# One decode step of attention and feed-forward on one core: GpSimd weighs and halves 32 of 128 rows of each value tile, VectorE sums the 16 that are left, and several matmuls become fewer and wider

## The chip, the core and the metric

The kernel runs on one core of a Trainium2 chip, in float32 throughout. The core has a matmul engine (TensorE, PE in the profile), VectorE (DVE), ScalarE (ACT), GpSimd (POOL) and SyncE (SP), which here only issues transfers, and 16 DMA engines that bring data from device memory to the on-chip memory SBUF. Results of matmuls go to PSUM. The metric is the device time of one execution in microseconds (us); lower is better.

## The reference

One token for each of four sequences goes through a block with adaptive layer norm: six modulation vectors come from a conditioning vector `c`; attention with 32 heads over a cache of 4096 keys and values per head; then a feed-forward with SiLU.

```python
mod = (_silu(c) @ w_mod).reshape(c.shape[0], 6, 1, -1)
sa, ca, ga, sb, cb, gb = (mod[:, i] for i in range(6))
h = _layernorm(x) * (1 + ca) + sa
q = (h @ wq).reshape(B, Sq, H, Dh).transpose(0, 2, 1, 3)
scores = einsum("bhqd,bhkd->bhqk", q, k_cache) * (Dh ** -0.5)
o = einsum("bhqk,bhkd->bhqd", softmax(scores), v_cache)
x = x + ga * (o.transpose(0, 2, 1, 3).reshape(B, Sq, H * Dh) @ wo)
h = _layernorm(x) * (1 + cb) + sb
x = x + gb * (_silu(h @ w1) @ w2)
```

Here B is 4, H is 32, the model is 512 wide, Dh is 128 and the cache has 4096 positions, so keys and values are 4 x 32 x 4096 x 128 numbers each, 268 MB each. The hidden layer is 1792 wide.

## The kernel before

The work on the cache is cut into 32 steps n, each for one sequence b = n mod 4 and one group t of four heads. A step has a key tile and a value tile of 128 partitions x 128 rows x 128 numbers, 8.4 MB each. A partition holds 128 consecutive positions of one head; "a row" below is one of these positions, 128 numbers in each partition.

**Transfers.** The pool `kv` has three buffers of the size of a tile. All big transfers go through the queue of SyncE, in the order `wm`, `wq`, k0, v0, k1, v1, ..., k31, v31, `wo`, and then `w1` and `w2` together in one buffer (`w12`). Each takes the buffer that was filled three places earlier, so k(n+1) waits until the work on v(n-1) is done, v(n+1) waits for the work on k(n), `wo` for the work on v30 and `w12` for the work on k31. SyncE issues in order: a transfer whose buffer isn't free holds back those behind it. `wo`, `w1` and `w2` come in pieces (`fetch`, L80).

**One step** (the loop at L353). The key tile is multiplied by the query in place: GpSimd does the first `NA` = 56 rows with a copy of the query in SBUF (`qw`), VectorE the other 72 with the query in PSUM (`qb`) (`mult`, L251). VectorE then adds up each row (`red`, L256), first its own 72 rows, then those of GpSimd; this gives 128 scores per partition in `sc`. Row maximum (`rowmax` L259, `bmax` L263, `negmax` L268) and exponential (`softexp` L275, on ScalarE) follow. GpSimd spreads the exponentials into two zero-padded tables `pz` (L281), 16 groups of four rows each, and TensorE multiplies them with the value tile (`pv`, L288): 32 matmuls of four rows, 512 columns, which run four at a time on four strips of 32 columns of the array. `po` collects two sequences b and b+1. The profile counts each float32 matmul as two passes, so a `pv` is 64.

`gather` (L306) masks `po` and adds up its four parts by four matmuls into `od`; it runs for the first pair in the step with b = 2 and for the second in the next step with b = 0. `spread` (L330) divides by the softmax sum and writes the result as weights `oz`, in steps with b = 0. `make_qb(n + 1)` (L240) makes the next query tile by ScalarE, a matmul and a copy. The engines get their instructions in exactly the order in which the code is written.

**The last step** (n = 31) has its key tile loaded in two halves, and GpSimd and VectorE multiply half by half, 28 and 36 rows each (L373 to L378).

**The end** (L401 to L442). `project` multiplies `oz` by `wo` into `accp`: for each t and each of four parts r there are four matmuls of 128 columns. The second pair's last `gather` and `spread` stand between its parts. Then come the gate and residual (L415, L416), a layer norm, 16 matmuls with `w1`, the SiLU, 56 matmuls with `w2` in the order of its six pieces, two operations for gate and residual, and the output's transfer. `busy` issues matmuls whose result isn't used.

**The start** (L177 to L236). `mods` makes the modulation vectors by 96 matmuls of 128 columns; the query projection with `wq` follows.

## Time and profile before

| | |
|---|---|
| time, median of 3 runs | 1323.78 us (1323.75 to 1323.86) |
| the profiled execution's own time | 1323.81 us |
| its span in the profile | 1321.9 us |
| busy: PE, DVE, ACT, POOL | 398.0, 923.3, 44.7, 533.5 us |
| mean granted TensorE clock | 0.636 of full speed |
| read from device memory | 567.30 MB |

The profile shows one execution, with times in us from the start of the span; the execution's own time has 1.9 us around that span. A group in the profile is a set of instructions of one source line (L252 is line 252), engine and operation, written as result <- operands; its columns are the busy time in all and the mean ns of one, then the engine's idle time ahead of them and what ended it. "PE" rows are matmul passes, "PEld" rows their weight loads, "SPq" rows the transfers that SyncE issues. A row of the timeline has the start, the duration from first to last, the engine, the line, the operation with its tiles and how many; square brackets give the idle time just before. The chain that ended last is followed back from the last instruction of the program.

### The profile page before, as it was taken

Reading aid. Unit: us, or ns where it says so; the run is one execution under the profiler, and the core shown is the slowest. Engines: PE = TensorE matmul, PEld = TensorE weight load, DVE = VectorE, ACT = ScalarE, POOL = GpSimd, SP = SyncE. Lnnn points to the kernel's source line nnn. Section 1 sums busy time; section 2 is a strip of 40 time slices with the busy share of each in tenths; the row PEclk is TensorE's granted clock in tenths of the full one; section 3 lists DMA queues with packets and bytes.
Section 4 is the critical chain, followed back from the end, with each engine's and each line's share of the span. In section 5 each row is a group of like instructions: output and inputs, shape, how many; then the busy total and the mean of one; then the engine's idle time right before and its main releaser. Section 6 shows DMA issues by size and latency. Waiting matters only on the chain.

```text
span 1321.9 us, 7059 instructions
## 1 busy us (share of the span) xinstructions
PE 398.0 (30%) x2998; PEld 145.4 (11%) x2998; DVE 923.3 (70%) x335; ACT 44.7 (3%) x146; POOL 533.5 (40%) x111
## 2 busy tenths in 40 slices
PE   3321223323123333212333321323332132333146
PEld 2100001101010010101001010100100010010014
DVE  1267877766887666788667678776668876676971
ACT  1100000000000000000000000000000000000000
POOL 1234455433445533354543334454334445433540
PEclk9765566665566666566666656666655666665569
DMA  9999999999999999999999999999999999999998
GB/s 414 441 418 439 442 419 438 439 424 431 441 430 429 437 436 427 436 436 429 435 433 435 428 435 438 426 435 440 423 435 444 418 437 444 419 437 439 420 422 330
DMA packets 12287, 567.76 MB, mean 430 GB/s; under 512 B 1440, under 2 KB 1504, under 8 KB 2272
## 3 DMA queue, kind: packets, MB, share of 16 engines
q1 hardware_dynamic: 12048, 567.29, 99.4%
q8 instruction: 23, 0.38, 0.1%
q14 instruction: 8, 0.07, 0.0%
q0 software_dynamic: 128, 0.01, 0.0%
q10 hardware_dynamic: 80, 0.02, 0.0%
HBM read 567.30 MB, written 0.01 MB: 429 GB/s over the span
## 4 chain that ended last, share of the span: by engine, by line
DMA 32%; issue 31%; POOL 25%; PE 7%; DVE 4%; POOLq 0%; SPq 0%; DVEq 0%
DMA k<-in_A_k_cache_dram 26%; POOL k L252 24%; PE po L297 6%; DMA w<-in_B_w_dram 3%; DMA wq<-in_A_wq_dram 3%; DVE sc L257 3%; DVE k L252 1%; POOL pz L281 1%; PE q L221 1%; PE mx L231 0%; POOLq L281 0%; DVE o L308 0%; PE po L434 0%; PE mx L265 0%; SPq L123 0%
## 5 line engine op out<-in xcount | busy, mean ns | idle before, releaser
L252 POOL TENSOR_TENSOR k<-k,qw 128x7168 f32<-128x7168 f32 (+1 forms) x33 | 491.4, 14893 | 290.1 <-DMA k<-in_A_k_cache_dram 264.7
L257 DVE TENSOR_REDUCE sc<-k 128x72 f32<-128x9216 f32 (+2 forms) x66 | 554.4, 8422 | 1.1
L252 DVE TENSOR_TENSOR k<-k,q 128x9216 f32<-128x9216 f32 (+1 forms) x33 | 312.3, 9463 | 309.3 <-DMA k<-in_A_k_cache_dram 300.1
L297 PE MATMUL po<-v,pz 128*32 128x512 f32 x2048 | 292.1, 735 | 48.6 <-POOL pz L281 47.9
L281 POOL TENSOR_TENSOR pz<-sc,hm 128x256 f32<-128x256 f32 x64 | 37.9, 612 | 458.1 <-ACT sc L279 445.7
L265 PE MATMUL mx<-ident,rm 128*128 128x128 f32 x32 | 14.5, 453 | 531.2 <-DVE rm L261 531.2
L314 PE MATMUL od<-o,spick 128*128 128x128 f32 x128 | 32.3, 431 | 293.4 <-DVE o L308 293.4
L297 PEld LDWEIGHTS po<-v,pz 128*32 128x32 f32 x2048 | 71.2, 132 | 248.2 <-issue 191.9
L265 PEld LDWEIGHTS mx<-ident,rm 128*128 128x128 f32 x32 | 5.8, 181 | 538.8 <-issue 332.1
L314 PEld LDWEIGHTS od<-o,spick 128*128 128x128 f32 x128 | 27.7, 319 | 296.5 <-DVE o L308 296.3
L279 ACT ACTIVATE sc<-sc,nm 128x128 f32<-128x128 f32 x32 | 12.8, 401 | 891.9 <-DVE nm L273 891.9
L270 DVE TENSOR_REDUCE hx<-mx 128x4 f32<-128x128 f32 x32 | 9.3, 291 | 19.7 <-PE mx L265 19.7
L247 ACT ACTIVATE qw<-q 128x128 f32<-128x128 f32 x32 | 8.9, 277 | 302.9 <-PE q L244 302.9
L308 DVE TENSOR_TENSOR o<-po,jm 128x512 f32<-128x512 f32 x16 | 10.9, 680 | 8.4 <-PE po L297 8.4
L244 PE MATMUL q<-qm,blk 128*128 128x128 f32 x64 | 15.6, 326 | 1.5 <-ACT qm L242 1.5
L183 PE MATMUL q<-wm 128*32 128x128 f32 x192 | 9.2, 375 | 20.3 <-DVE wm L170 20.3
L244 PEld LDWEIGHTS q<-qm,blk 128*128 128x128 f32 x64 | 9.5, 188 | 27.0 <-issue 25.1
L242 ACT ACTIVATE qm<-qn,sel 128x128 f32<-128x128 f32 x32 | 12.4, 387 | 0.9 <-DMA xg<-in_A_x_dram 0.9
L221 PE MATMUL q<-wq,wm 128*32 128x512 f32 x64 | 9.3, 748 | 7.4 <-DMA wq<-in_A_wq_dram 7.4
L183 PEld LDWEIGHTS q<-wm 128*32 128x32 f32 x192 | 7.8, 153 | 21.0 <-DVE wm L170 20.3
L261 DVE TENSOR_REDUCE rm<-sc 128x1 f32<-128x128 f32 x32 | 9.1, 284 | 0.9
L167 DVE SCALAR_TENSOR_TENSOR wm<-wm 128x128 f32<-128x128 f32 x1 | 0.3, 291 | 12.3 <-ACT wm L166 12.3
(79 smaller groups left out, 104.2 us busy)
## 6 DMA issues: line engine op xcount, KB each, us to landing
k<-in_A_k_cache_dram SPq DMA_DIRECT2D x2, 4096.0 KB
wm<-in_w_mod_dram SPq DMA_DIRECT2D x1, 6144.0 KB
wo<-in_A_wo_dram SPq DMA_DIRECT2D x1, 4096.0 KB
wo<-in_A_wo_dram SPq DMA_DIRECT2D x1, 2048.0 KB
wo<-in_A_wo_dram SPq DMA_DIRECT2D x2, 1024.0 KB, 35.2
...
```

Source lines behind the costliest of these rows:

```text
L183: nc.tensor.matmul(p[W * g : W * (g + 1), u, :], csT[:, k, :], wmt[:, k, o : o + P], start=k == 0, stop=k == NK - 1,)
L221: nc.tensor.matmul(pq[i][W * g : W * (g + 1), :], hT[:, k, :], wqt[:, k, ch * CW : (ch + 1) * CW], start=k == 0, stop=k == NK - 1,)
L242: nc.scalar.activation(m, qn, AF.Copy, scale=sel[:, n : n + 1])
L244: nc.tensor.matmul(p, blk.rearrange("p i x -> p (i x)"), m, start=True, stop=True)
L252: eng.tensor_mul(kt[n][:, lo:hi, :], kt[n][:, lo:hi, :], src[n].unsqueeze(1).to_broadcast([P, hi - lo, Dh]))
L257: nc.vector.tensor_reduce(sc[n][:, lo:hi], kt[n][:, lo:hi, :], axis=AX.X, op=ALU.add)
L265: nc.tensor.transpose(p, nm[n].to_broadcast([P, P]), ident)
L279: nc.scalar.activation(sc[n], sc[n], AF.Exp, bias=nm[n], accum_out=rs[t][:, b : b + 1])
L281: nc.gpsimd.tensor_mul(pz[h][:, : HG * W].rearrange("p (g x) -> p g x", g=HG)[:, :, E:].rearrange("p g (i j) -> p g i j", i=HP), sc[n][:, ...
L297: nc.tensor.matmul(po[t, q][W * g : W * (g + 1), :], pz[h][:, o : o + W], vt[n][:, JJ * j : JJ * (j + 1), :].rearrange("p j d -> p (j d)") ...
L308: nc.vector.tensor_mul(o, po[t, q].rearrange("p (j d) -> p j d", j=JJ), jm.unsqueeze(2).to_broadcast([P, JJ, Dh]))
L314: nc.tensor.matmul(od[t], spick[:, 2 - 2 * q : 2 - 2 * q + P], o[:, j, :], start=(q == 0 and j == 0), stop=(q == 1 and j == JJ - 1),)
```

## The change

On the value side, GpSimd multiplies the first `NV` = 32 rows of a value tile by their exponentials in place and adds rows 16 to 31 to rows 0 to 15 (`vmult`, `fold`). In the next step VectorE adds up these 16 rows with a strided view (`vsum`), and one matmul puts the sum into `po`. `pv` then has 24 matmuls instead of 32, and `pz` holds 24 groups. The last step (`first(n)` is 0) does without this. On the key side GpSimd has 48 rows instead of 56; in the last step it has 32 in each half.

`make_qb` makes four query tiles at once with one matmul of 512 columns every fourth step. `gather` adds its four parts on VectorE and has one matmul. `project` has one matmul of 512 columns for each t and r, the four r on four strips; the strips are then added up by four matmuls with `sel`, for which `accp` is copied by VectorE and ScalarE. `mods` is likewise turned to 512 columns with a masking step behind it. The table for the SiLU is loaded ahead by a one-column activation, and one `busy` matmul goes.

```diff
-    NA = 56
+    NA = 48
+    NL = 64
+    NV = 32
...
     def mods(dsts, i):
...
+        n = len(dsts)
+        p = psum([P, D], "q", 2)
+        for k in range(NK):
+            for u in range(n):
+                nc.tensor.matmul(
+                    p[W * u : W * (u + 1), :], csT[:, k, :], wmt[:, k, (i + u) * D : (i + u + 1) * D],
+                    start=k == 0, stop=k == NK - 1,
+                )
+        z = psum([P, n, P], "q", 2)
+        r = W * n
+        for g in range(G):
+            m = mm[:r, g % 2, :n, :]
+            nc.vector.tensor_mul(
+                m, p[:r, g * P : (g + 1) * P].unsqueeze(1).to_broadcast([r, n, P]),
+                hm[:r, :n].unsqueeze(2).to_broadcast([r, n, P]),
+            )
+            nc.tensor.matmul(z[W * g : W * (g + 1), :, :], sel[:r, :], m, start=True, stop=True)
...
     def make_qb(n):
-        m = work.tile([P, Dh], F32, tag="lnu", name=f"qm{n}", bufs=1)
-        nc.scalar.activation(m, qn, AF.Copy, scale=sel[:, n : n + 1])
-        p = psum([P, Dh], "q", 2)
-        nc.tensor.matmul(p, blk.rearrange("p i x -> p (i x)"), m, start=True, stop=True)
-        qb[n] = p
+        if n % B == 0:
+            m = work.tile([P, B, Dh], F32, tag="o", name=f"qm{n}", bufs=1)
+            for b in range(B):
+                nc.scalar.activation(m[:, b, :], qn, AF.Copy, scale=sel[:, n + b : n + b + 1])
+            p = psum([P, B, Dh], "q", 2)
+            nc.tensor.matmul(p, blk.rearrange("p i x -> p (i x)"), m, start=True, stop=True)
+            for b in range(B):
+                qb[n + b] = p[:, b, :]
...
+    def first(n):
+        return NV // JJ if n < N - 1 else 0
+
+    def vmult(n):
+        if first(n):
+            nc.gpsimd.tensor_mul(
+                vt[n][:, :NV, :], vt[n][:, :NV, :], sc[n][:, :NV].unsqueeze(2).to_broadcast([P, NV, Dh])
+            )
+            fold(nc.gpsimd, n, NV // 2)
+
+    def fold(eng, n, m):
+        eng.tensor_add(vt[n][:, :m, :], vt[n][:, :m, :], vt[n][:, m : 2 * m, :])
+
+    def vsum(n):
+        t, b = divmod(n, B)
+        q, a = divmod(b, 2)
+        s = work.tile([P, Dh], F32, tag="lnu", name="vs", bufs=1)
+        nc.vector.tensor_reduce(s, vt[n][:, : NV // 2, :].rearrange("p j d -> p d j"), axis=AX.X, op=ALU.add)
+        o = (1 - a) * E
+        nc.tensor.matmul(po[t, q][0:W, 0:Dh], hs[:, o : o + W], s, start=False, stop=a == 1)
...
-        for j in range(NG):
+        f = first(n)
+        for j in range(f, NG):
...
-        for j in range(JJ):
-            nc.tensor.matmul(
-                od[t], spick[:, 2 - 2 * q : 2 - 2 * q + P], o[:, j, :],
-                start=(q == 0 and j == 0), stop=(q == 1 and j == JJ - 1),
-            )
+        s = work.tile([P, Dh], F32, tag="lnu", name="s", bufs=1)
+        nc.vector.tensor_reduce(s, o.rearrange("p j d -> p d j"), axis=AX.X, op=ALU.add)
+        nc.tensor.matmul(od[t], spick[:, 2 - 2 * q : 2 - 2 * q + P], s, start=q == 0, stop=q == 1)
...
-                for g in range(G):
-                    nc.tensor.matmul(
-                        accp[W * g : W * g + B, :], oz[:, t, r, :], wot[:, t, r, g * P : (g + 1) * P],
-                        start=(t == 0 and r == 0), stop=(t == NT - 1 and r == R - 1),
-                    )
+                nc.tensor.matmul(
+                    accp[W * r : W * r + B, :], oz[:, t, r, :], wot[:, t, r, :],
+                    start=t == 0, stop=t == NT - 1,
+                )
...
             make_qb(n + 1)
+            if n:
+                vsum(n - 1)
             red(n, NA, NJ)
         else:
             for lo in (0, NJ // 2):
-                mid, hi = lo + NA // 2, lo + NJ // 2
+                mid, hi = lo + NL // 2, lo + NJ // 2
                 mult(nc.gpsimd, qw, n, lo, mid)
                 mult(nc.vector, qb, n, mid, hi)
+                if lo == 0:
+                    vsum(n - 1)
                 red(n, mid, hi)
-            red(n, NJ // 2, NJ // 2 + NA // 2)
...
-        red(n, 0, NA if n + 1 < N else NA // 2)
+        if n + 1 < N:
+            red(n, 0, NA)
+        else:
+            for lo in (0, NJ // 2):
+                red(n, lo, lo + NL // 2)
...
+        vmult(n)
         pv(n)
...
-    nc.vector.tensor_mul(x1, ga, accp)
+    ac = work.tile([P, D], F32, tag="o", name="ac", bufs=1)
+    nc.vector.tensor_copy(ac[:, : D // 2], accp[:, : D // 2])
+    nc.scalar.activation(ac[:, D // 2 :], accp[:, D // 2 :], AF.Copy)
+    xa = psum([P, P], "mx", 2)
+    for g in range(G):
+        nc.tensor.matmul(xa[W * g : W * (g + 1), :], sel, ac[:, g * P : (g + 1) * P], start=True, stop=True)
+    nc.vector.tensor_mul(x1, ga, xa)
     nc.vector.tensor_add(x1, x1, xg)
     busy(4)
     layernorm_mod(hg, x1, sb, cb1)
+    nc.scalar.activation(th[:, 0:1], x1[:, 0:1], AF.Tanh)
...
-    busy(6)
+    busy(5)
```

Two places show how the order of instructions changes. The first is VectorE from the softmax of step 30 to the row maximum of step 31; k31 and v30 are the key tile of step 31 and the value tile of step 30, sc31 the scores, q the query in PSUM, vs the sum of the 16 rows. Before:

```order
L273 TENSOR_REDUCE nm30_2309<-hx30_2306 128x1
L252 TENSOR_TENSOR k31_2281<-k31_2281,q_2289 128x4608
L257 TENSOR_REDUCE sc31_2354<-k31_2281 128x36
L252 TENSOR_TENSOR k31_2281<-k31_2281,q_2289 128x4608
L257 TENSOR_REDUCE sc31_2354<-k31_2281 128x36
L257 TENSOR_REDUCE sc31_2354<-k31_2281 128x28 x2
L261 TENSOR_REDUCE rm31_2363<-sc31_2354 128x1
```

The same place on VectorE after the change:

```order
L292 TENSOR_REDUCE nm30_2081<-hx30_2078 128x1
L271 TENSOR_TENSOR k31_2055<-k31_2055,q_1879 128x4096
L326 TENSOR_REDUCE vs_2123<-v30_2027 128x128
L276 TENSOR_REDUCE sc31_2120<-k31_2055 128x32
L271 TENSOR_TENSOR k31_2055<-k31_2055,q_1879 128x4096
L276 TENSOR_REDUCE sc31_2120<-k31_2055 128x32 x3
L280 TENSOR_REDUCE rm31_2132<-sc31_2120 128x1
```

The sum over v30 now stands behind the first multiplication of step 31, ahead of every reduction and of the second multiplication.

The second place is GpSimd from the key rows of step 30 to the end of step 31; pz0 and pz1 are the two tables, qw the query in SBUF, hm a constant mask. Before:

```order
L252 TENSOR_TENSOR k30_2222<-k30_2222,qw30_2231 128x7168
L281 TENSOR_TENSOR pz0_118<-sc30_2284,hm_101 128x16x16
L281 TENSOR_TENSOR pz1_119<-sc30_2284,hm_101 128x16x16
L252 TENSOR_TENSOR k31_2281<-k31_2281,qw31_2291 128x3584 x2
L281 TENSOR_TENSOR pz0_118<-sc31_2354,hm_101 128x16x16
L281 TENSOR_TENSOR pz1_119<-sc31_2354,hm_101 128x16x16
```

The same place on GpSimd after the change:

```order
L271 TENSOR_TENSOR k30_2003<-k30_2003,qw30_2008 128x6144
L302 TENSOR_TENSOR pz0_118<-sc30_2058,hm_101 128x8x16
L302 TENSOR_TENSOR pz1_119<-sc30_2058,hm_101 128x16x16
L314 TENSOR_TENSOR v30_2027<-v30_2027,sc30_2058 128x4096
L320 TENSOR_TENSOR v30_2027<-v30_2027 128x2048
L271 TENSOR_TENSOR k31_2055<-k31_2055,qw31_2061 128x4096 x2
L302 TENSOR_TENSOR pz0_118<-sc31_2120,hm_101 128x16x16
L302 TENSOR_TENSOR pz1_119<-sc31_2120,hm_101 128x16x16
```

The weighing and the halving of v30 (4096 and 2048 elements per partition) now stand between the tables of step 30 and the key rows of step 31; each earlier step has the same two instructions at this place.

More of the change, by code (lines that the diff above doesn't have):

```diff
@@ L107 @@
     tmp = s0.take(P)
+    mm = s0.take(2, 4, P)
     csT, hT = s0.take(NK, W), s0.take(NK, W)
@@ L160 @@
         nc.gpsimd.memset(t, 0.0)
+    hs = const.tile([P, W + E], F32, name="hs")
+    nc.vector.memset(hs, 0.0)
+    nc.vector.tensor_copy(
+        hs[:, E : 2 * E].rearrange("p (i j) -> p i j", i=HP), hm.unsqueeze(2).to_broadcast([P, HP, JJ])
+    )
     oz = const.tile([P, NT, R, B], F32, name="oz")
@@ L177, in mods @@
     def mods(dsts, i):
-        p = psum([P, 4, P], "q", 2)
-        for u in range(len(dsts)):
-            for k in range(NK):
-                for g in range(G):
-                    o = (i + u) * D + g * P
-                    nc.tensor.matmul(
-                        p[W * g : W * (g + 1), u, :], csT[:, k, :], wmt[:, k, o : o + P],
-                        start=k == 0, stop=k == NK - 1,
-                    )
+        n = len(dsts)
[15 more added lines that the diff above has]
+            nc.tensor.matmul(z[W * g : W * (g + 1), :, :], sel[:r, :], m, start=True, stop=True)
         for u, d in enumerate(dsts):
             nc.scalar.activation(
-                d, p[:, u, :], AF.Copy,
+                d, z[:, u, :], AF.Copy,
                 scale=0.25 if i + u == 5 else 0.5, bias=1.0 if i + u in (1, 4) else 0.0,
@@ L240, in make_qb @@
     def make_qb(n):
[L241 to L245 removed]
+        if n % B == 0:
[6 more added lines that the diff above has]
+                qb[n + b] = p[:, b, :]
         qw[n] = work.tile([P, Dh], F32, tag="qw", name=f"qw{n}")
[L247 removed]
+        nc.scalar.activation(qw[n], qb[n], AF.Copy)
     sc, nm, po, rs = {}, {}, {}, {}
@@ L300, in pv @@
                 vt[n][:, JJ * j : JJ * (j + 1), :].rearrange("p j d -> p (j d)"),
-                start=(a == 0 and j < G), stop=(a == 1 and j >= NG - G),
+                start=(a == 0 and j < f + G), stop=(a == 1 and j >= NG - G and (g > 0 or not f)),
             )
@@ L337, in spread @@
         nc.vector.tensor_copy(oz[:, t], ot[:, :, :B])
-    accp = psum([P, P], "acc", 1)
+    accp = psum([P, D], "acc", 1)
     nc.vector.memset(accp, 0.0)
@@ L344, in project @@
             for r in range(R):
-                for g in range(G):
-                    nc.tensor.matmul(
-                        accp[W * g : W * g + B, :], oz[:, t, r, :], wot[:, t, r, g * P : (g + 1) * P],
-                        start=(t == 0 and r == 0), stop=(t == NT - 1 and r == R - 1),
-                    )
+                nc.tensor.matmul(
+                    accp[W * r : W * r + B, :], oz[:, t, r, :], wot[:, t, r, :],
+                    start=t == 0, stop=t == NT - 1,
+                )
     make_qb(0)
@@ L405 @@
     project(NT - 1, NT)
+    x1, hg, y = (s2.take(P) for _ in range(3))
+    h2T, hid, th, hidT = s2.take(NK, W), s2.take(FG), s2.take(FG), s2.take(NI, W)
     idle = psum([P, P], "q", 2)
@@ L411, in busy @@
             nc.tensor.matmul(idle, ident, qn, start=True, stop=True)
-    x1, hg, y = (s2.take(P) for _ in range(3))
-    h2T, hid, th, hidT = s2.take(NK, W), s2.take(FG), s2.take(FG), s2.take(NI, W)
-    nc.vector.tensor_mul(x1, ga, accp)
+    ac = work.tile([P, D], F32, tag="o", name="ac", bufs=1)
[5 more added lines that the diff above has]
+    nc.vector.tensor_mul(x1, ga, xa)
     nc.vector.tensor_add(x1, x1, xg)
```

11 lines of the change are left out of this document (6 added, 5 removed).

## The prediction

> **What bounds the kernel now.** I first read the head of the page for the load of the DMA engines (the row "DMA" is their busy share in 40 slices, the last row the queue of SyncE).
>
> ```profile
> span 1321.9 us, 7059 instructions
> DMA  9999999999999999999999999999999999999998
> q1 hardware_dynamic: 12048, 567.29, 99.4%
> ```
>
> The queue keeps the 16 engines busy for 99.4% of the span, in every stretch. 567.29 MB in 1321.9 us is 429 GB/s. No compute engine sets the pace as long as this queue never runs dry. Next, the end of the chain that ended last (start, duration, what).
>
> ```profile
> 1304.65 13.11 DMA w<-in_B_w_dram
> 1317.81 0.47 PE po L434 x8
> ```
>
> The last piece of `w2` lands at 1317.8, eight matmul passes follow, and the span ends 3.62 us after the last of them ends (1318.28). The change neither removes a byte nor touches these last steps. So nothing here can become faster by more than a fraction of a microsecond, and two questions remain: does the queue still never run dry, and does the compute of the last step still end before the last piece lands?
>
> The timeline tells how much room there is: one step in the middle (step 14 starts at 601), the start, and the step ahead of the last.
>
> ```profile
> 38.38 9.33 PE L221 MATMUL q<-wq,wm 128*32 128x512 f32 x64 [7.36 <-DMA wq<-in_A_wq_dram]
> 47.77 0.33 SPq L82 DMA_DIRECT2D v<-in_A_v_cache_dram  x1
> 57.81 9.75 DVE L252 TENSOR_TENSOR k<-k,q 128x9216 f32<-128x9216 f32 x1 [30.58 <-DMA k<-in_A_k_cache_dram]
> ...
> 601.20 0.33 SPq L82 DMA_DIRECT2D k<-in_A_k_cache_dram  x1
> 620.60 0.68 DVE L308 TENSOR_TENSOR o<-po,jm 128x512 f32<-128x512 f32 x1
> 628.84 0.33 SPq L82 DMA_DIRECT2D v<-in_A_v_cache_dram  x1
> 628.84 0.29 DVE L261 TENSOR_REDUCE rm<-sc 128x1 f32<-128x128 f32 x1
> 631.04 1.18 POOL L281 TENSOR_TENSOR pz<-sc,hm 128x256 f32<-128x256 f32 x2 [14.57 <-ACT sc L279]
> ...
> 1222.31 9.76 DVE L252 TENSOR_TENSOR k<-k,q 128x9216 f32<-128x9216 f32 x1 [10.46 <-DMA k<-in_A_k_cache_dram]
> ```
>
> From step 0 (57.81) to step 30 (1222.31) a step takes 1164.5 / 30 = 38.82 us, two tiles of 19.4 us. With T as the landing of k(n), k(n+1) has to be issued before v(n) has landed, T + 19.4, and v(n+1) before k(n+1) has, T + 38.8. Before, they were issued at 601.20, about T, and at 628.84, T + 27.6.
>
> **The change, part by part.** Prices come from the groups by shape (busy us, mean ns).
>
> ```profile
> L252 DVE TENSOR_TENSOR k<-k,q 128x9216 f32<-128x9216 f32 x31 | 302.4, 9754 | 309.3 <-DMA k<-in_A_k_cache_dram 300.1 <-ACT qw L247 9.2
> L257 DVE TENSOR_REDUCE sc<-k 128x56 f32<-128x7168 f32 x31 | 235.9, 7608 | 0.0
> L257 DVE TENSOR_REDUCE sc<-k 128x28 f32<-128x3584 f32 x2 | 7.7, 3876 | 0.0
> L252 POOL TENSOR_TENSOR k<-k,qw 128x7168 f32<-128x7168 f32 x31 | 475.8, 15350 | 290.1 <-DMA k<-in_A_k_cache_dram 264.7 <-PE po L297 16.8 <-PE q L244 8.6
> L252 POOL TENSOR_TENSOR k<-k,qw 128x3584 f32<-128x3584 f32 x2 | 15.6, 7816 | 0.0
> L281 POOL TENSOR_TENSOR pz<-sc,hm 128x256 f32<-128x256 f32 x64 | 37.9, 612 | 458.1 <-ACT sc L279 445.7 <-issue 12.4
> ```
>
> VectorE takes (9754 - 7608) / 16 = 134 ns a row, multiplying or adding: 80 rows 10.83 us, 48 rows 6.54, 32 rows 4.41. GpSimd takes (15350 - 7816) / 28 = 269 ns a row: 48 rows 13.20, 32 rows 8.89, and the halving of 16 rows 7.82 - 12 x 0.269 = 4.59. `vmult` with its fold is 13.48 us, the smaller tables are 0.31 + 0.61 = 0.92.
>
> The reduction over 16 rows by a view of stride 512 bytes isn't in the trace. Three small reductions of 128 elements bound it: `hm` reads side by side, `jm` and `sel` with strides of 16 and 128 bytes.
>
> ```profile
> L140 DVE TENSOR_REDUCE hm<-ident 128x4 f32<-128x128 f32 x1 | 0.3, 279 | 0.0
> L144 DVE TENSOR_REDUCE jm<-ident 128x4 f32<-128x128 f32 x1 | 0.4, 368 | 0.0
> L135 DVE TENSOR_REDUCE sel<-ident 128x32 f32<-128x128 f32 x1 | 0.4, 376 | 3.2 <-POOL ident masks.py:199 3.2
> ```
>
> Side by side it would cost 2048 x 1.05 + 145 = 2.30 us; the strided rows add 89 and 97 ns per 128 elements, some 0.73 ns each, hence 2048 x 1.78 + 145, about 3.75 us. I take 3.75, since those rows have a stride too, and keep 2.30 as the other end. The same prices give `gather`'s new reduction of 512 elements 1.07 (0.68 at best).
>
> The Trainium skill, "SBUF — State Buffer", section "Door 1: The DMA port swizzle", says that reads which stay within a 16-byte line run at full rate and each step to another line is penalised. The rows agree: 16 and 128 bytes cost alike. By that rule the time is the one with 3.75; by a price that ignores strides it would be the one with 2.30, 1333.6 (below).
>
> Steady steps. GpSimd ends the fold of v(n-1) only after T, and `vsum` waits for it. From one fold to the next: vsum 3.75, 80 rows 10.83, 48 rows 6.54, row maximum to tables 2.20 (628.84 to 631.04), tables 0.92, vmult and fold 13.48, in all 37.72. Every fourth step (b = 2) adds a `gather` of 0.68 + 1.07 = 1.75, and every fourth (b = 0) a `gather` and a `spread` of 0.83 (1295.36 to 1296.26 in the rows below, without its gaps), 2.58. The mean is 38.80, against 38.82 of the transfers: VectorE and GpSimd alternate in a loop that just fits. VectorE is in its own multiplication until T + 10.83, so the fold lies under it up to there. Walked through four steps, the fold ends at most at T + 12.3; vsum then ends at T + 16.1 and k(n+1) is issued, 3.3 us ahead of its limit. v(n+1) goes at about T + 34, 5 us ahead. The queue doesn't run dry, and the steady steps cost nothing; their cover is these 3.3 us. `pv`'s eight saved matmuls, `make_qb` and `gather`'s saved matmuls lie beside this loop and gain nothing.
>
> The start costs nothing either. The query projection waited 7.36 us for `wq`, which takes most of the longer `mods`; v0's issue at 47.77 can slip by several microseconds before k0 has landed (57.8).
>
> The end carries the sum. These rows show it before.
>
> ```profile
> 1278.96 0.28 DVE L261 TENSOR_REDUCE rm<-sc 128x1 f32<-128x128 f32 x1
> 1281.30 1.18 POOL L281 TENSOR_TENSOR pz<-sc,hm 128x256 f32<-128x256 f32 x2 [12.36 <-issue]
> 1281.97 8.77 PE L297 MATMUL po<-v,pz 128*32 128x512 f32 x64 [0.16 <-POOL pz L281]
> 1289.28 0.12 PEld L297 LDWEIGHTS po<-v,pz 128*32 128x32 f32 x4 [0.31 <-issue]
> 1289.71 0.12 PEld L297 LDWEIGHTS po<-v,pz 128*32 128x32 f32 x4 [0.31 <-issue]
> 1294.16 1.16 PE L314 MATMUL od<-o,spick 128*128 128x128 f32 x8
> 1295.36 0.35 DVE L332 TENSOR_SCALAR on<-od,rd 128x128 f32<-128x128 f32 x1 [3.85 <-PE od L314]
> 1296.09 0.17 DVE L337 COPY oz<-ot 128x16 f32<-128x16 f32 x1
> 1301.58 0.29 DVE L415 TENSOR_TENSOR w<-mod,acc 128x128 f32<-128x128 f32 x1 [5.32 <-PE acc L346]
> 1305.50 2.46 PE L424 MATMUL q<-w 128*32 128x448 f32 x24 [0.15 <-DVE w L170]
> 1309.04 0.96 PE L424 MATMUL q<-w 128*32 128x448 f32 x8 [1.07 <-DMA w<-in_B_w_dram]
> 1310.10 1.28 ACT L166 ACT_TABLE_LOAD   x1 [5.67 <-PE q L424]
> 1311.39 0.54 ACT L166 ACTIVATE w<-q 128x448 f32<-128x448 f32 x1
> 1313.62 1.95 PE L434 MATMUL po<-w 128*32 128x128 f32 x64 [2.09 <-DVE w L170]
> ```
>
> Step 30 starts at 1222.31. The fold of step 28 ends 10.83 + 37.72 + 2.58 - 38.82 = 12.31 into step 29, that of step 29 11.21 into step 30. The fold of v30 thus ends at 1222.31 + 11.21 + 37.72 + 1.75 = 1272.99. VectorE has multiplied its first rows of k31 by then (some 1262) and stands at `vsum`, with all of k31's other work queued behind it. Then: vsum 3.75, a reduction, a multiplication, three reductions, five times 4.41 = 22.05 (GpSimd's two halves, 17.78, end at 1290.8, in time), so 1298.79 where it was 1278.96. `pv` of step 31 follows 2.34 + 0.67 later and takes 8.77: it ends at 1310.57 instead of 1290.74, 19.8 us later.
>
> From there to the last `w2` matmul: 0.1; `project` up to t = 3, 32 passes of 512 columns, at 0.43 us for four (the weight loads above), 3.43; `gather`'s matmul 0.35; t = 4 to 6, 2.58; t = 7, 0.86; the copies and four `sel` matmuls 1.05 (an estimate: 8 passes took 0.47 at 1317.81, the rest is for the copies and waits); gate, residual and layer norm 3.92 (1301.58 to 1305.50); `w1` 3.2 (2.46 + 0.96 without the wait's pipeline); 0.1; SiLU 2.23 (1311.39 to 1313.62, its table of 1.28 now loaded earlier); `w2` 112 passes at 1.95 / 64, 3.41. Sum 21.2, so 1331.8, against 1318.28 before. Without its waits for transfers the same stretch of before was 1.7 us longer (`project` and `gather`'s matmul 1.64, as the row below shows for `project`'s 7.7; the table 1.28; less the 1.05 and small gaps), so it could have ended at 1290.74 + 22.9 = 1313.6: it had 4.7 us of cover behind the transfers, and the 19.8 less 1.7 use that up and leave some 13.5.
>
> ```profile
> L346 PE MATMUL acc<-wo,oz 128*4 128x128 f32 x256 | 7.7, 273 | 2.2 <-DMA wo<-in_A_wo_dram 1.5 <-issue 0.7
> ```
>
> `wo` (issued at 1276.8) and `w12` (1298.8) still go out before v31 and `wo` have landed (1222.31 + 38.8 + 19.4 = 1280.5 and 1299.9), so the weights aren't late.
>
> The span becomes 1331.8 + 3.62 = 1335.4 and the time, by the profiled execution's 1.9 us around the span (1323.81, which is the median within 0.03), **1337.3 us**. With 2.30 and 0.68 for the reductions, the fold of v30 ends at 1222.31 + 10.83 + 36.27 + 1.36 = 1270.77, `pv` at 1306.9, and the time is 1333.6.
>
> **The rivals.** No change, 1323.8: the transfers still end last. `pv` of step 31 would have to end by about 1297, 13 us earlier than my sum has it. Even with a free `vmult` and fold, VectorE's 22.05 us and vsum from 1262 on would end at 1288 and `pv` at 1300. Only far lower prices on both engines would do. Chance 0.07.
>
> A loop longer than the transfers, slower still: if vsum or GpSimd's weighing (with the broadcast score as operand) costs 1 us more, the loop is 39.8; each step falls 1 us behind, and from 3.3 us on the queue runs dry, so about 28 - 3 = 25 us go there and some 4 more in the tail: 1366. It decides from 0.15 us a step on. For it: the mean of 38.80 against 38.82. Against it: I took the dearer price of vsum, and GpSimd's 15350 ns already hold both kinds of neighbour, VectorE's multiplication for 9.75 us and its reduction after that. Chance 0.18.
>
> Faster, about 1320: the tail behind the last piece would have to shrink by most of its 3.62 us, or the transfers run faster with fewer matmuls reading SBUF. The DMA row is 9 in slices with and without `pv`. Chance 0.01. The Trainium skill, "SBUF — State Buffer", section "Who interferes with whom", keeps engine ports and DMA ports apart; this trace agrees, with 99.4%.
>
> **How the numbers follow.** My forecast, the last step's end behind the transfers, has 0.74. Less price for the strided view and a somewhat quicker tail reach down to 1329; a loop up to 0.45 us too long (28 x 0.45 - 3.3 = 9 dry, plus 4) up to 1350. This leaves out the no-change case and the worse half of the long loop, under 0.2. A difference below 0.2% (2.6 us) can't be told from none here: faster 0.01, same 0.07, slower 0.92.
>
> **What would show it.** In the profile after: the first `vsum` after k31's first multiplication preceded by some 10 us of VectorE idle, released by GpSimd's fold; `vsum` at 3.7 us rather than 2.3; fold at 4.6 and `vmult` at 8.9; `w` landing at 1317 to 1319 with the last `w2` matmuls some 13 us later, released by VectorE and no longer by a DMA. Steps 38.8 us apart show the loop fits; a DMA row with 8s in the middle would show the long loop. If `pv` of step 31 ends before 1300, my sum is wrong.

## The result and the profile after

| | before | after |
|---|---|---|
| time, median (lowest to highest) of 6 runs each | 1323.80 us (1323.75 to 1323.86) | 1338.15 us (1334.85 to 1341.2) |
| ratio, 95% interval | | 1.0106 (1.009 to 1.0123) |
| the profiled execution: its time, its span | 1323.81, 1321.9 us | 1334.85, 1332.0 us |

The kernel became 14.35 us slower, where 13.5 were predicted. One thing stands out ahead of any row: the six executions of before lie within 0.11 us, those of after within 6.4 us. The profiled execution of after is the shortest of its six, 3.3 us under their median; its rows show the part of the loss that every execution has, and the experiments the part that varies.

The head of the page shows that the queue still works without a pause up to the last slice. Its share is lower since the span goes on after the last transfer.

```profile
span 1332.0 us, 5396 instructions
DMA  9999999999999999999999999999999999999995
q1 hardware_dynamic: 12048, 567.29, 98.8%
```

The new operations, from the groups by shape (busy us, mean ns of one, idle time ahead):

```profile
L271 DVE TENSOR_TENSOR k<-k,q 128x10240 f32<-128x10240 f32 x31 | 335.4, 10821 | 151.2 <-DMA k<-in_A_k_cache_dram 151.2
L314 POOL TENSOR_TENSOR v<-v,sc 128x4096 f32<-128x4096 f32 x31 | 218.0, 7033 | 0.0
L320 POOL TENSOR_TENSOR v<-v 128x2048 f32<-128x2048 f32 x31 | 140.3, 4526 | 2.4
L326 DVE TENSOR_REDUCE vs<-v 128x128 f32<-128x2048 f32 x31 | 113.4, 3658 | 8.9 <-POOL v L320 8.9
L271 POOL TENSOR_TENSOR k<-k,qw 128x4096 f32<-128x4096 f32 x2 | 17.6, 8840 | 0.0
L357 DVE TENSOR_REDUCE s<-o 128x128 f32<-128x512 f32 x16 | 16.3, 1020 | 0.5
```

`vsum` (L326) is idle 8.9 us in all of its 31 turns, so in 30 of them it never waits for the fold: the steady loop fits. Step 14 in the timeline, with T = 600.93:

```profile
600.93 10.82 DVE L271 TENSOR_TENSOR k<-k,q 128x10240 f32<-128x10240 f32 x1 [5.54 <-DMA k<-in_A_k_cache_dram]
604.09 4.53 POOL L320 TENSOR_TENSOR v<-v 128x2048 f32<-128x2048 f32 x1
611.67 3.66 DVE L326 TENSOR_REDUCE vs<-v 128x128 f32<-128x2048 f32 x1
615.39 0.33 SPq L84 DMA_DIRECT2D k<-in_A_k_cache_dram  x1
634.19 0.33 SPq L84 DMA_DIRECT2D v<-in_A_v_cache_dram  x1
640.37 10.82 DVE L271 TENSOR_TENSOR k<-k,q 128x10240 f32<-128x10240 f32 x1 [4.58 <-DMA k<-in_A_k_cache_dram]
```

The fold ends at T + 7.7, under VectorE's own multiplication. k(n+1) is requested at T + 14.5, 4.9 us before v(n) is due to land (T + 19.4); before, it was requested at about T. And this step took 39.44 us, although VectorE stood 4.58 us waiting for its key tile.

The end, in the timeline:

```profile
1221.81 10.82 DVE L271 TENSOR_TENSOR k<-k,q 128x10240 f32<-128x10240 f32 x1 [5.58 <-DMA k<-in_A_k_cache_dram]
1256.60 4.42 DVE L271 TENSOR_TENSOR k<-k,q 128x4096 f32<-128x4096 f32 x1
1258.27 7.03 POOL L314 TENSOR_TENSOR v<-v,sc 128x4096 f32<-128x4096 f32 x1
1269.91 3.65 DVE L326 TENSOR_REDUCE vs<-v 128x128 f32<-128x2048 f32 x1 [8.90 <-POOL v L320]
1295.36 0.29 DVE L280 TENSOR_REDUCE rm<-sc 128x1 f32<-128x128 f32 x1
1298.31 8.43 PE L340 MATMUL po<-v,pz 128*32 128x512 f32 x64
1325.06 3.26 PE L489 MATMUL po<-w 128*32 128x128 f32 x112 [1.05 <-DVE w L178]
```

VectorE has done its first multiplication of k31 at 1261.0 and stands 8.9 us at `vsum` until GpSimd has folded v30. Everything else of k31 is queued behind that: the row maximum comes at 1295.36 (1278.96 before), `pv` ends at 1306.74 (1290.74 before). The last `w2` matmuls run in one piece of 112, released by VectorE, where the last eight waited for a transfer before. The table by stretches (the last two columns are the DMA share and GB/s) shows that the transfers were done by then, at about 1316.5:

```profile
1314.00:1319.00 5.00, 3.68 (x33) 2.83 (x30) 2.64 (x10) 2.35 (x4) 0.00 (x0) 1.00 0.51 194
1319.00:1325.00 6.00, 4.86 (x45) 2.27 (x44) 1.97 (x3) 1.61 (x3) 0.00 (x0) 1.00 0.01 3
```

### The profile page after: what moved, and what is told of

Same layout as the page of the kernel before. It is cut to its first block, busy times and chain, and to the rows that moved or that the text cites. A ratio compares the mean times of both kernels' runs of the same rounds, so it can differ in the third digit from the quotient of the medians.

```text
span 1332.0 us, 5396 instructions
## 1 busy us (share of the span) xinstructions
PE 340.9 (26%) x2106; PEld 99.2 (7%) x2106; DVE 1084.8 (81%) x393; ACT 45.3 (3%) x148; POOL 817.1 (61%) x173
## 4 chain that ended last, share of the span: by engine, by line
DMA 58%; issue 25%; DVE 11%; PE 4%; POOL 2%; ACT 0%; ACTq 0%; SPq 0%; DVEq 0%; POOLq 0%
DMA k<-in_A_k_cache_dram 57%; DVE vs L326 8%; POOL k L271 1%; DVE sc L276 1%; DMA wm<-in_c_dram 1%; PE q L190 1%; PE po L340 1%; PE q L237 1%; PE acc L386 1%; POOL v L314 1%; POOL v L320 0%; PE q L202 0%; PE po L489 0%; PE q L479 0%; DVE wm L198 0%
## 5 line engine op out<-in xcount | busy, mean ns | idle before, releaser
L276 DVE TENSOR_REDUCE sc<-k 128x80 f32<-128x10240 f32 (+1 forms) x66 | 554.0, 8418 | 0.1
L271 DVE TENSOR_TENSOR k<-k,q 128x10240 f32<-128x10240 f32 (+1 forms) x33 | 344.3, 10433 | 151.2 <-DMA k<-in_A_k_cache_dram 151.2
L271 POOL TENSOR_TENSOR k<-k,qw 128x6144 f32<-128x6144 f32 (+1 forms) x33 | 425.8, 12906 | 52.9 <-DMA k<-in_A_k_cache_dram 52.9
L302 POOL TENSOR_TENSOR pz<-sc,hm 128x128 f32<-128x128 f32 (+1 forms) x64 | 31.2, 509 | 425.5 <-ACT sc L298 425.5
L340 PE MATMUL po<-v,pz 128*32 128x512 f32 x1552 | 239.1, 781 | 44.1 <-POOL pz L302 44.0
L314 POOL TENSOR_TENSOR v<-v,sc 128x4096 f32<-128x4096 f32 x31 | 218.0, 7033 | 0.0
L320 POOL TENSOR_TENSOR v<-v 128x2048 f32<-128x2048 f32 x31 | 140.3, 4526 | 2.4
L326 DVE TENSOR_REDUCE vs<-v 128x128 f32<-128x2048 f32 x31 | 113.4, 3658 | 8.9 <-POOL v L320 8.9
L284 PE MATMUL mx<-ident,rm 128*128 128x128 f32 x32 | 14.5, 453 | 407.6 <-DVE rm L280 407.6
L328 PE MATMUL po<-vs,hs 128*32 128x128 f32 x62 | 19.7, 420 | 320.8 <-DVE vs L326 320.8
L357 DVE TENSOR_REDUCE s<-o 128x128 f32<-128x512 f32 x16 | 16.3, 1020 | 0.5
```

The lines of the kernel that those rows point to most:

```text
L271: eng.tensor_mul(kt[n][:, lo:hi, :], kt[n][:, lo:hi, :], src[n].unsqueeze(1).to_broadcast([P, hi - lo, Dh]))
L276: nc.vector.tensor_reduce(sc[n][:, lo:hi], kt[n][:, lo:hi, :], axis=AX.X, op=ALU.add)
L284: nc.tensor.transpose(p, nm[n].to_broadcast([P, P]), ident)
L302: nc.gpsimd.tensor_mul(pz[h][:, f * W : HG * W].rearrange("p (g x) -> p g x", g=m)[:, :, E:].rearrange("p g (i j) -> p g i j", i=HP), sc[n ...
L314: nc.gpsimd.tensor_mul(vt[n][:, :NV, :], vt[n][:, :NV, :], sc[n][:, :NV].unsqueeze(2).to_broadcast([P, NV, Dh]))
L320: eng.tensor_add(vt[n][:, :m, :], vt[n][:, :m, :], vt[n][:, m : 2 * m, :])
```

## The experiments

Each group of four shared a chip and the runs of the kernel before on it (1323.76, 1323.90 and 1323.82 us). The theory was that of the prediction: the wait for v30's fold in the last step makes the loss. The rivals: the wider matmuls or the end's order make it; or the steady steps do, through the transfers. T is the start of VectorE's multiplication of a step.

**x1_same**: the changed kernel itself again.

> The changed kernel once more, since its six executions spread over 6 us where those of before spread over 0.1. Theory (the end of the compute is bare, and TensorE's granted clock in it differs from execution to execution): times between 1334 and 1342; in a profile of a slower execution the row maximum of step 31 still stands at about 1295.4, and the stretch from pv of step 31 to the last w2 matmul is longer than the 30.05 us of the first profile, with a lower granted clock there. Rival (the steady loop sometimes runs the queue dry): the row maximum of step 31 stands later by what the time is longer, and w lands after 1318.

1335.01 us (1333.67 to 1338.7), ratio 1.0089 (1.0075 to 1.0103). Its profiled span is 1333.8, 1.8 us more than in the first profile. Step 30 starts at 1223.01 instead of 1221.81, which is 1.2 of it; the last `pv` takes 9.03 us instead of 8.43, the other 0.6. So these two executions differ ahead of step 30, in the transfers, and less at the end: the row maximum of step 31 moved too (1296.56), which the theory of the clock had standing still. Their times differ by only 0.7 us, so the pair alone doesn't explain a scatter of 6 us; the later starts of step 30 in two related kernels below (1225.87 in x2_skip30, 1226.81 in y4_narrow_tail) point the same way.

**x2_skip30**: step 30 does without the weighing too.

```diff
     def first(n):
-        return NV // JJ if n < N - 1 else 0
+        return NV // JJ if n < N - 2 else 0
...
-                if lo == 0:
+                if lo == 0 and first(n - 1):
                     vsum(n - 1)
```

> Step 30 too goes without weighing and halving on GpSimd, as step 31 does; all else as changed. Theory (VectorE stands at the sum over v30 until GpSimd has weighed and halved v30, and the transfers no longer hide the end): row maximum of step 31 at about 1283 instead of 1295.4, its pv ends at 1294, 21.6 us on is 1316, before the last piece of w2 lands, so 1323.8 to 1325. Rival (the wide matmuls and the strip sums make the end long): 1333 or more. Rival (fewer key rows on GpSimd): at least 5 us above before, 1329 or more.

1326.36 us (1324.53 to 1328.7), ratio 1.0018 (1.0009 to 1.0027). Of the 11.25 us that the changed kernel loses on this chip, 8.65 go with the weighing of v30, and with it VectorE's wait and sum in the last step. The end of its chain of waits:

```profile
1308.43 13.89 DMA w<-in_B_w_dram
1322.36 0.47 PE po L489 x8
```

The transfers end last again, but their last piece lands at 1322.3 where it was 1317.8 before. The same bytes came later, by 4.5 us in this execution and 2.6 us in the median, with a spread of 4.2 us. That was not expected.

**x3_late**: in the last step `vsum` stands behind the second multiplication instead of ahead of the first reduction.

```diff
                 mult(nc.vector, qb, n, mid, hi)
-                if lo == 0:
+                if lo:
                     vsum(n - 1)
```

> In step 31 VectorE's sum over v30 is moved behind the reduction of its first rows and the multiplication of its second; all else as changed. Theory: the idle 8.9 us ahead of that sum are filled with 8.8 us of work, the transfer of wo goes out at the same 1273.6, the row maximum comes when GpSimd's second half is done and reduced, at 1292 instead of 1295.4, so 3.5 us less than the changed kernel, about 1334.6. Rivals by which the wait of VectorE is not on the path: no difference, 1338.

1332.28 us (1331.51 to 1335.76), ratio 1.0072 (1.0059 to 1.0084): 2.7 us less than x1_same, where 3.5 were expected. The ranges of the two overlap, so the times alone don't settle it; the rows do. The row maximum of step 31 comes 70.2 us after the start of step 30 (1293.42 less 1223.26) instead of 73.6, the 3.4 us that were expected, and in this execution the last `pv` takes 10.01 us, which gives 1.6 of it back. VectorE's wait for the fold is gone, but another takes part of its place (timeline):

```profile
1271.41 3.65 DVE L326 TENSOR_REDUCE vs<-v 128x128 f32<-128x2048 f32 x1
1280.21 4.42 DVE L276 TENSOR_REDUCE sc<-k 128x32 f32<-128x4096 f32 x1 [0.82 <-POOL k L271]
1288.97 4.42 DVE L276 TENSOR_REDUCE sc<-k 128x32 f32<-128x4096 f32 x1 [4.34 <-POOL k L271]
```

GpSimd starts its halves of k31 only when v30 is folded, so VectorE waits 0.82 + 4.34 us for those instead of 8.90 for the fold. With either order the last step pays for the weighing of v30.

**x4_wide_only**: no weighing, and the old shares of the key rows; the wider matmuls stay.

```diff
-    NA = 48
-    NL = 64
+    NA = 56
+    NL = 56
...
     def first(n):
-        return NV // JJ if n < N - 1 else 0
+        return 0
```

(and `vsum` only where `first(n - 1)` isn't 0)

> Only the fewer, wider matmuls (modulation, query tiles, gather, project with the strips' sum, early table): no weighing on GpSimd and no sum on VectorE in any step, 56 key rows on GpSimd as before. Theory: the transfers end last again, 1323.8, and in the profile pv of step 31 ends at 1290 to 1291 and the stretch behind it would take 21.6 us, hidden. Rival (the wide matmuls make the end long): 1327 or more.

1324.42 us (1324.2 to 1324.69), ratio 1.0005 (0.9996 to 1.0014). Behind the transfers the wider matmuls gain nothing and cost at most the 0.66 us by which this median lies above 1323.76; the rest of the loss belongs to the weighing and to the rows that were moved for it. The moved rows alone don't make it, since x2_skip30 above and z1_sum_after below keep them.

**y1_late_issue** asks about the transfers alone. It is the kernel before, with nothing weighed and no row moved; only a read of one row of v(n-1), whose result isn't used, stands in the middle of VectorE's reduction, so that k(n+1) has to wait for it.

```diff
+    def peek(n):
+        s = work.tile([P, 1], F32, tag="pk", name="pk", bufs=1)
+        nc.vector.tensor_reduce(s, vt[n][:, 0, :], axis=AX.X, op=ALU.max)
...
-            red(n, NA, NJ)
+            red(n, NA, NA + 36)
+            if n:
+                peek(n - 1)
+            red(n, NA + 36, NJ)
```

> The kernel before with one addition: VectorE's reduction of its 72 rows is cut in two (36 and 36), and between the parts it reads one row of v(n-1), result unused. This frees v(n-1) and sends k(n+1) out at T + 14.9 instead of T, about where the changed kernel sends it, without any weighing, strided sum or wide matmul. Theory (the steady transfers lose 1 to 4 us because each key tile is now requested only some 4.5 us ahead of its turn): 1325 to 1327, executions spread by over 1 us, some 64 KB packets over 2.6 us long around T + 16 to T + 20. Rival (GpSimd's weighing or VectorE's strided reads disturb the transfers): 1323.8 to 1324.2, spread 0.3 us, packets as before.

1338.14 us (1332.46 to 1342.22), ratio 1.0102 (1.0083 to 1.0122): the direction was as expected, the size many times larger. The profiled execution is one of the shorter ones (1333.7). A 0.28 us read and a late request cost as much as the whole change. Step 14 in the timeline:

```profile
605.33 9.75 DVE L252 TENSOR_TENSOR k<-k,q 128x9216 f32<-128x9216 f32 x1 [10.43 <-DMA k<-in_A_k_cache_dram]
619.99 0.28 DVE L306 TENSOR_REDUCE pk<-v 128x1 f32<-128x128 f32 x1
620.33 0.33 SPq L82 DMA_DIRECT2D k<-in_A_k_cache_dram  x1
```

The request goes out at T + 15.0, 4.4 us ahead of its turn, and VectorE waits 10.43 us for the tile: the compute has plenty of room. In the chain of waits the requests follow each other now, each from the release of the buffer to the landing:

```profile
112.23 23.73 DMA k<-in_A_k_cache_dram
151.04 23.63 DMA k<-in_A_k_cache_dram
501.73 25.11 DMA k<-in_A_k_cache_dram
```

23.7 + 15.0 is the 38.7 of a step; where it takes 25 us, the next request is later by the same amount and nothing is caught up. The table by stretches shows how this looks from the queue, here first for before, then for y1_late_issue:

```profile
60.00:1200.00 1140.00, 323.05 (x2069) 106.80 (x2069) 840.73 (x261) 30.93 (x116) 492.66 (x88) 0.62 1.00 433
```

```profile
60.00:1200.00 1140.00, 321.96 (x2069) 105.92 (x2069) 841.20 (x317) 30.93 (x116) 487.34 (x88) 0.62 1.00 430
```

The busy share is 1.00 in both. What fell is the rate, from 433 to 430 GB/s: 0.7% of 1140 us, 7.9 us, and step 30 starts 8.9 us later (1231.25 against 1222.31). A queue that never looks idle can still be slowed.

The trace keeps a record of each packet that the DMA engines moved, and these show where the time went. Of some 7,690 packets of 64 KB in the 30 steps, with a median of 2.42 us, 24 took over 2.6 us before and 230 in y1_late_issue (up to 4.33 us). Of the 230, 207 start between T + 16 and T + 21.1, shortly behind the request and around the landing of v(n); before has none there. What the long packets take above 2.42 us, shared among 16 engines, is 8.0 us against 0.75 before, most of the 8.2 us by which the 30 steps are longer. The expectation had named such packets at this place.

**y2_early**: x2_skip30, with `vsum` after 60 of the 80 rows of the multiplication, for an earlier request.

```diff
-            mult(nc.vector, qb, n, NA, NJ)
-            make_qb(n + 1)
+            mult(nc.vector, qb, n, NA, NA + 60)
             if n:
                 vsum(n - 1)
+            mult(nc.vector, qb, n, NA + 60, NJ)
+            make_qb(n + 1)
```

> As the kernel in which step 30 too goes without weighing (1326.4), but in each other step VectorE's sum over v(n-1) stands after 60 of its 80 rows of multiplication, so that k(n+1) goes out at about T + 11.9 instead of T + 14.5. Theory (late request): 1324.2 to 1325.2, less spread, fewer long packets. Rival (the weighing itself disturbs the transfers): 1326.4 as there.

1344.29 us (1343.83 to 1345.55), ratio 1.0155 (1.0141 to 1.0168). The expectation failed (timeline):

```profile
607.59 8.15 DVE L271 TENSOR_TENSOR k<-k,q 128x7680 f32<-128x7680 f32 x1 [2.47 <-DMA k<-in_A_k_cache_dram]
618.37 3.66 DVE L326 TENSOR_REDUCE vs<-v 128x128 f32<-128x2048 f32 x1 [2.63 <-POOL v L320]
621.95 2.81 DVE L271 TENSOR_TENSOR k<-k,q 128x2560 f32<-128x2560 f32 x1
622.09 0.33 SPq L84 DMA_DIRECT2D k<-in_A_k_cache_dram  x1
```

The other 20 rows (2.81 us) now stand between one `vsum` and the next fold, inside the loop of VectorE and GpSimd. That was 35.74 us (3.66 + 10.81 + 6.54 + 2.20 + 0.97 + 7.03 + 4.53) and on average 1.05 for `gather` and `spread`; with 2.81 it is 39.6, more than the 38.7 of the transfers. So the fold came late, `vsum` waited 2.63 us for it, and the request went out at T + 14.5 after all.

**y3_nv40**: 40 rows weighed instead of 32.

```diff
-    NV = 32
+    NV = 40
```

> The changed kernel with 40 instead of 32 value rows on GpSimd. With the measured prices one round from fold to fold is vsum 4.54, 80 rows 10.81, 48 rows 6.54, softmax 2.20, tables 0.93, weighing 8.79, fold 5.66, sum 39.47, and 1.05 more on average for gather and spread, 40.5 in all against 38.78 of the transfers. Theory (GpSimd and VectorE alternate in a loop that decides as soon as it is longer than two tiles): the queue runs dry from about step 3 on, 28 x 1.74 = 49 us and some 8 in the tail, about 1390. Rival (the engines overlap more than this loop says): 1337 to 1342, only the tail longer.

1383.84 us (1383.62 and 1384.06), ratio 1.0452 (1.0434 to 1.047), near the 1390 of the loop and far from the rival. The group of `vsum`, and the stretch as above:

```profile
L326 DVE TENSOR_REDUCE vs<-v 128x128 f32<-128x2560 f32 x31 | 140.2, 4521 | 61.8 <-POOL v L320 61.7
```

```profile
60.00:1200.00 1140.00, 259.93 (x1368) 70.54 (x1368) 972.19 (x290) 31.37 (x114) 795.38 (x141) 0.58 0.98 418
```

Here `vsum` waits for the fold in the steady steps, the DMA share falls to 0.98 and the rate to 418 GB/s. This is the long loop that the prediction had as a rival, and what it looks like; the change itself doesn't have it.

**y4_narrow_tail**: the changed kernel with `gather`, `project` and the gate as before, and without the early table load. One run.

```diff
-        s = work.tile([P, Dh], F32, tag="lnu", name="s", bufs=1)
-        nc.vector.tensor_reduce(s, o.rearrange("p j d -> p d j"), axis=AX.X, op=ALU.add)
-        nc.tensor.matmul(od[t], spick[:, 2 - 2 * q : 2 - 2 * q + P], s, start=q == 0, stop=q == 1)
+        for j in range(JJ):
+            nc.tensor.matmul(
...
-                nc.tensor.matmul(
-                    accp[W * r : W * r + B, :], oz[:, t, r, :], wot[:, t, r, :],
...
+                for g in range(G):
+                    nc.tensor.matmul(
+                        accp[W * g : W * g + B, :], oz[:, t, r, :], wot[:, t, r, g * P : (g + 1) * P],
...
-    nc.vector.tensor_mul(x1, ga, xa)
+    nc.vector.tensor_mul(x1, ga, accp)
...
-    nc.scalar.activation(th[:, 0:1], x1[:, 0:1], AF.Tanh)
```

> The changed kernel with the gather, project, gate and table load of before (128-column matmuls, no strip sum, no early table). The end of compute is bare, so the wide forms can be weighed: from the end of pv of step 31 to the last w2 matmul 22.9 us against 21.6 in the changed kernel, so 1 to 2 us longer. Rival (the wide matmuls are what makes the end late): shorter than 21.6.

1339.18 us, span 1337.3. The last `pv` and the last `w2` matmuls in its timeline:

```profile
1302.28 8.52 PE L340 MATMUL po<-v,pz 128*32 128x512 f32 x64
1330.40 3.26 PE L485 MATMUL po<-w 128*32 128x128 f32 x112 [2.31 <-DVE w L178]
```

From the end of the last `pv` to the end of the last `w2` matmul it takes 22.9 us (1310.80 to 1333.66), against 21.6 in after (1306.74 to 1328.32) and in x1_same (1308.53 to 1330.11): the prediction had 22.9 and 21.2. So the wider matmuls save 1.3 us at a bare end. The rest of the difference lies ahead of step 30 again, which starts at 1226.81.

The last four ask how early a request has to be. **z1_sum_after** is x2_skip30 with 16 rows weighed.

```diff
-    NV = 32
+    NV = 16
```

> As the kernel in which step 30 too goes without weighing, but with 16 value rows on GpSimd instead of 32, so that VectorE sums 8. The sum stands behind VectorE's multiplication as in the changed kernel; k(n+1) goes out at about T + 12.7, 6.6 us ahead of its turn instead of 4.9. Theory (a request that comes too short ahead of its turn costs the transfers): between 1324 and 1325.5, less spread than with 32 rows (1326.4, spread 4.2). Rival (weighing on GpSimd or strided sums disturb the transfers): about half of the 2.6 us goes, 1325.

1324.37 us (1324.1 to 1324.76), ratio 1.0005 (0.9996 to 1.0013), as expected. x4_wide_only, with the same wide matmuls and nothing weighed, was 0.66 us above its kernel before, so the 0.55 us here leave nothing for the request. It goes out at T + 12.7 (timeline):

```profile
600.70 10.82 DVE L271 TENSOR_TENSOR k<-k,q 128x10240 f32<-128x10240 f32 x1 [7.34 <-DMA k<-in_A_k_cache_dram]
613.39 0.33 SPq L84 DMA_DIRECT2D k<-in_A_k_cache_dram  x1
```

**z2_sum_first** is z1_sum_after with `vsum` ahead of the step's multiplication.

```diff
         if n + 1 < N:
+            if n:
+                vsum(n - 1)
             mult(nc.gpsimd, qw, n, 0, NA)
             mult(nc.vector, qb, n, NA, NJ)
             make_qb(n + 1)
-            if n:
-                vsum(n - 1)
```

> The same work on every engine as with 16 rows and the sum behind the multiplication, only that VectorE's sum over v(n-1) stands ahead of the multiplication of step n, where VectorE waits for the key tile anyway; k(n+1) goes out at T + 2 or before, over 15 us ahead. Theory (late request): 1323.8 to 1324.5, executions within 0.6 us of one another. Rival (the work itself disturbs the transfers): as with the sum behind the multiplication, within 0.3 us.

1365.61 us (1365.39 to 1366.34), ratio 1.0317 (1.0303 to 1.0331). This expectation failed as that of y2_early had. The wait ahead of `vsum` shows it:

```profile
619.72 1.98 DVE L326 TENSOR_REDUCE vs<-v 128x128 f32<-128x1024 f32 x1 [7.79 <-POOL v L320]
621.62 10.81 DVE L271 TENSOR_TENSOR k<-k,q 128x10240 f32<-128x10240 f32 x1
```

The whole multiplication of 10.81 us now stands in the loop: 1.98 + 10.81 + 10.82 + 6.54 + 2.20 + 1.07 + 3.61 + 2.37 = 39.40, with 1.05 some 40.4. That is 1.6 more than the 38.82 of a step before, 47 over 30 steps; step 30 starts 46.4 us later than before, and the time is 41.8 us longer. The multiplication ahead of `vsum` is what gives GpSimd its time.

**z3_peek_early** is y1_late_issue with the same read right behind the multiplication.

```diff
             make_qb(n + 1)
+            if n:
+                peek(n - 1)
             red(n, NA, NJ)
```

> The kernel before with VectorE's unused read of one row of v(n-1) right behind its multiplication, so that k(n+1) goes out at T + 10.1, 9.3 us ahead of its turn (3.9 us ahead it took 1338). Theory (late request): 1323.8 to 1324.6, spread under 0.6 us. Rival (the additional read or wait on VectorE costs by itself): 1330 or more.

1323.94 us (1323.67 to 1324.24), ratio 1.0001 (0.9992 to 1.001), as expected.

```profile
601.50 9.76 DVE L252 TENSOR_TENSOR k<-k,q 128x9216 f32<-128x9216 f32 x1 [10.38 <-DMA k<-in_A_k_cache_dram]
611.51 0.33 SPq L82 DMA_DIRECT2D k<-in_A_k_cache_dram  x1
```

The same read, the same chain of requests, 5 us earlier, and nothing is lost. It isn't the read that costs in y1_late_issue; it is when the request goes out. (The 3.9 us in the expectation are 4.4 in the rows of y1_late_issue.) This pair separates the request from the weighing, which z1_sum_after, with half the weighing, doesn't.

**z4_warm**: the changed kernel with 44 unused matmuls behind the last `vsum`, to keep TensorE's clock up for the end.

```diff
                     vsum(n - 1)
+                    wp = psum([P, P], "q", 2)
+                    for _ in range(44):
+                        nc.tensor.matmul(wp, ident, qn, start=True, stop=True)
```

> The changed kernel with 44 unused matmuls on TensorE behind the sum over v30 in step 31, where it waits for some 20 us, so that its granted clock is up when pv of step 31 starts. Theory (the bare end also pays for a clock that starts at half): pv of step 31 takes 6.9 to 7.1 instead of 8.4 to 10.0, time 1.5 to 3 us less than the changed kernel, about 1333, its spread left as it is, since that comes from the transfers. Rival (clock without weight): 1335 to 1338.

1336.37 us (1334.42 to 1338.17), ratio 1.0093 (1.0078 to 1.0109), between the two medians of the changed kernel, where 1333 was expected. It tells nothing of the clock (timeline):

```profile
1277.12 11.62 PE L423 MATMUL q<-qn,ident 128*128 128x128 f32 x88
1301.24 8.54 PE L340 MATMUL po<-v,pz 128*32 128x512 f32 x64
```

The added matmuls were over at 1288.7, 12.5 us before the last `pv`, which took 8.54 us as it had without them (8.43 and 9.03). The granted clock was low again by then: 0.55 in the first 3.4 us of that `pv`, then 1.00. In after it was 0.55 in the first 3.1 us of the 8.43; at 1.00 throughout that `pv` would take some 1.4 us less, an estimate that no run here tests.

In one table, from the timelines, the packet records and the runs. "Ahead" is T + 19.4 less the request of k(n+1); the third column is the time from the start of step 0 to that of step 30 in the profiled execution, the fourth counts the 64 KB packets of over 2.6 us in that time:

| kernel | ahead, us | 30 steps, us | long packets | median, us | highest less lowest |
|---|---|---|---|---|---|
| before | 17 to 21 | 1164.5 | 24 | 1323.8 | 0.1 to 1.1 |
| x4_wide_only | 16 to 20 | 1164.7 | 24 | 1324.42 | 0.5 |
| z3_peek_early | 9.4 | 1164.1 | 24 | 1323.94 | 0.6 |
| z1_sum_after | 6.7 | 1163.2 | 28 | 1324.37 | 0.7 |
| x2_skip30 | 4.9 | 1167.6 | 132 | 1326.36 | 4.2 |
| after; x1_same | 4.9 | 1163.9; 1164.6 | 64; 73 | 1338.15; 1335.01 | 6.4; 5.0 |
| x3_late | 4.9 | 1165.3 | 84 | 1332.28 | 4.3 |
| y4_narrow_tail; z4_warm | 4.9 | 1168.5; 1166.5 | 123; 112 | 1339.18; 1336.37 | one run; 3.8 |
| y1_late_issue | 4.4 | 1172.7 | 230 | 1338.14 | 9.8 |

With 6.7 us or more the 30 steps take the 1163 to 1165 us of the kernels at the top. With 4.9 us they take 0 to 4 us more, differently in each execution, and with 4.4 us 8 more; the number of long packets rises with that in all but one pair. The medians of the kernels that weigh v30 (after, x1_same, x3_late, y4_narrow_tail, z4_warm) hold the wait in the last step too. Value tiles show the same order within one execution: in x2_skip30, counted from 1 to 7 us behind the request in steps 2 to 28, 27 key tiles requested 4.9 us ahead have 95 long packets, 14 value tiles requested 5.4 us ahead of their turn (T + 38.7 less T + 33.3) have 11, and 13 requested 7.1 us ahead have one.

No version was faster than the kernel before: its queue is full from the start to 1317.8, and no experiment removes bytes.

## Why the prediction was right, and where two of its steps were not

**The last step.** "VectorE stands at `vsum`, with all of k31's other work queued behind it": shown by the rows of after and by x2_skip30, which takes the weighing of v30 away and gets back 8.65 of 11.25 us. That the transfers then end last again, as the first theory has it, stands in its chain.

**The prices.** `vsum` 3.66 (predicted 3.75, though its own product is 3.79), the fold 4.53 (4.59), `gather`'s reduction 1.02 (1.07), VectorE's 80 rows 10.82 (10.83): as taken. The strided view was to cost 1.78 or 1.05 ns an element; 3658 ns for 2048 and 1895 for 1024 (z1_sum_after) make 1.72. By the Trainium skill, "SBUF — State Buffer", section "Door 1: The DMA port swizzle", each step to another 16-byte line is penalised; the measured time is the one with that penalty.

**The term that was mis-sized** is "`vmult` with its fold is 13.48 us". The fold was right; `vmult` was priced like GpSimd's key rows, at 8.89 us, and took 7.03. The key multiplication takes 8840 / 4096 = 2.16 ns an element, the fold 4526 / 2048 = 2.21, `vmult` 7033 / 4096 = 1.72 (1.71 with 40 rows, 8747 ns for 5120). In `vmult` one operand stays the same along a whole row; in the other two both change with each element. What VectorE does meanwhile makes no difference: the fold takes 4.53 us under its multiplication and 4.50 in the last step, where it stands still. So by these rows GpSimd's price goes with the operand's view, which the sum didn't allow for. The consequence, in the profiled execution: the fold of v30 ends 48.1 us after the start of step 30 instead of 50.7, the row maximum comes at 1295.36 instead of 1298.79, `pv` ends at 1306.74 instead of 1310.57. With the 21.6 us behind it (21.2 predicted) the span is 1332.0 instead of 1335.4.

**"The steady steps cost nothing; their cover is these 3.3 us" failed.** The loop fits, better than worked out: 35.74 + 1.05 = 36.8 of 38.7 us, and `vsum` never waits. The request is earlier than forecast too, 4.9 us ahead of its limit instead of 3.3. Yet the transfers became slower and varied from one execution to the next. The step treated every request made before its turn as equal; the runs show that it isn't so, and that the cost begins between 6.7 and 4.9 us ahead: a few packets around the landing of v(n) take longer than the usual 2.42 us, up to 4.33 in y1_late_issue. In the profiled execution of after, the 30 steps happened to take no longer than before, so their length alone would not have shown it. In the median it is some 3 us, an estimate: 1338.15 against the 1334.85 of that execution, or the 2.6 us that x2_skip30 keeps.

The two errors have opposite signs: 3.4 us too long at the end and some 3 too short in the transfers. A third is smaller: the profiled execution has 2.85 us around its span where 1.9 were taken, so its time is 1334.85. That 1337.3 came out so near to 1338.15 is luck. The mechanism that was forecast makes about three quarters of the loss, not all of it.

**The rivals.** No change: `pv` of step 31 ends at 1306.74, not before 1300. The long loop: not in the change (`vsum` waits 0.0 in 30 of 31 steps), but shown to be real at 40 rows, where it costs 60 us, and in z2_sum_first. Faster through fewer matmuls: 268 us of PE instead of 323 between 60 and 1200 left the rate at 433 GB/s. The 99.4% with which the prediction saw transfers and engines undisturbed can't show this, since that share also stays where a queue is slowed.

**Open.** Why packets around the landing of v(n) take longer when the next request comes 4 to 5 us ahead of its turn. One thought is that the 16 engines don't finish v(n) together and that with a short lead each tile waits for the last of them; most of the lost time shows as longer packets, though, not as pauses between them, and no run here tests a cause. What TensorE's clock costs at the bare end is an estimate only (z4_warm).
